# A hash-attention and gated feed-forward kernel: third pair's loads on the SP ring, a dummy matmul per step of the first block, one more PSUM copy on VectorE, the last output tile in two halves

## The chip, the cores and the metric

The kernel runs on one core of a Trainium2 chip. The metric is the device time of one execution in microseconds (us). A profiled span, which is what the trace covers, is about 2 us shorter than the time of the same execution. Each execution also reports the mean clock that the throttle granted to TensorE (1.0 is full speed).

Executions of one kernel do not agree here to a fraction of a per cent. In three sets of timed runs of the kernel before (157 executions) they lie between 359.7 and 368.2 us, and the mean clock goes with it: some 360.9 us where it is above 0.9925, 362.5 near 0.99, 364.3 near 0.98. Executions more than 1.5% above the fastest of the same kernel are labelled slow (48 of the 157); the ratios below use the fast ones only. The slow ones of the kernel before are, with few exceptions, those with the lowest clocks (0.959 to 0.984), so leaving them out also leaves out part of what a steadier clock is worth.

## The reference

```python
# q, k, v: (4, 8, 768, 64); proj: (64, 6)
q_bucket = sum over bits of ((q @ proj) > 0) * 2**bit        # the same for k
mask = q_bucket[..., :, None] == k_bucket[..., None, :]
attn = softmax(where(mask, q @ k.T / sqrt(64), -1e9))
x = (attn @ v), heads joined                                  # (3072, 512)
ffn = (gelu(x @ w_gate) * (x @ w_val)) @ w_out
out = x + sigmoid(x @ w_res) * ffn                            # (3072, 512), float32
```

## The kernel before

Attention works through 16 pairs of heads (4 batches by 4 pairs). For a pair, q and k are transposed on TensorE (tiles `tps`), hashed by small matmuls (`hps`), and the signs are written by VectorE (`bits`). Seven "hash rows" per operand are then moved by DMA under the scaled q and k in the tile `aug`, so that a score matmul over 64 + 7 = 71 rows gives a large negative number where the hashes differ. A step is two score matmuls (`sc`), one exp on ScalarE (`e`), and six matmuls with v (`av`, over 65 columns). 24 steps make a block; six steps belong to one pair. After each block comes the feed-forward of its tokens, whose matmuls fill TensorE during the next block. The first block has nothing to fill it with.

```python
    load_pair(1, nc.sync, "qk")          # SP ring
    load_pair(0, nc.sync, "v")
    load_pair(1, nc.sync, "v")
    ...
    def prep_pair(n):                    # pairs 1 to 3
        for g in range(3):
            ps = mm_psum.tile([P, 512], FP32, tag="mm", name="tps")
            for i in range(4):
                nc.tensor.transpose(ps[:, i * P:(i + 1) * P], tiles[4 * g + i], ident)
            if g == 1 and n > 1:
                nc.vector.tensor_copy(trT[:, g * 512:(g + 1) * 512], ps)
            else:
                nc.scalar.copy(trT[:, g * 512:(g + 1) * 512], ps)
            yield True
        ...                              # hash matmuls, bits on VectorE
        for i in range(4):               # the hash rows, by DMA
            eng = nc.sync
            eng.dma_start(a[D:KAUG, i // 2, (i % 2) * S:(i % 2 + 1) * S], bits[32 * i:32 * i + NR])
        ...
    prep_first()
    cast_v(0)                            # GpSimd: v of pair 0 to bf16
    load_pair(2, nc.gpsimd)              # the third pair
    prep = prep_pair(1)
    ...
    load_pair(3, nc.gpsimd)
    cast_v(1)
    for _ in range(KM):
        run(weights)                     # GpSimd issues weight loads; more at pairs 2 and 3
    for i in range(NS + LEAD):
        scores(i)                        # cut: conditions
        ...                              # attend(i - 2), prepare, feed-forward pieces
```

`mm_psum` has three buffers (in PSUM, where this kernel's matmuls write and ScalarE and VectorE read) for all transposes, hashes and feed-forward products; the last output tile is 12 matmuls of 512 columns, two VectorE operations and one DMA.

## Time and profile before

| | before |
|---|---|
| median time of three executions | 363.50 us (361.92 to 363.65) |
| profiled span, mean clock | 362.8 us, 0.971 |
| TensorE busy | 350.9 us, 97% |
| score step 6, step 12, step 18 start | 21.78, 29.35, 34.72 us |
| gate matmuls (`gps`) of the first block follow each other without a wait ("run free") from | 45.08 us |
| from there to the last matmul's start | 312.5 us |
| last matmul's end to the end of the span | 4.85 us |

The last four rows split the span into a head, a middle and a tail. In the middle TensorE is busy nearly throughout (312.78 of 312.91 us in this profile), and it is the same to 0.3 us in ten of the fourteen profiles of this study (312.5 to 312.8 us; the other four are those with weights held back); head and tail are where the time can move. The prediction below shows the lines that this rests on. In the chain of waits, a line is the start in us, the length in us, and what the chain went through: an instruction, a transfer (DMA), or "issue". In the tables of stretches the columns are the stretch, its length, the busy time of PE, PEld, DVE, ACT and POOL with instruction counts, the granted clock, and the DMA share and GB/s.

### The profile page before, as it was taken

How to read it: one execution, taken by the hardware profiler on the slowest of the kernel's cores; microseconds unless marked ns; L12 is line 12 of the kernel's file. 1: busy time of each engine (PE TensorE's matmuls, PEld its weight loads, DVE VectorE, ACT ScalarE, POOL GpSimd, SP SyncE). 2: the span in 40 equal slices, each digit the busy share in tenths (PEclk: the TensorE clock that was granted, in tenths of full speed). 3: DMA queues.
4: the chain of work that ended last, by engine and by line, in shares of the span. 5: the costliest groups of instructions: out<-in, count | busy, mean ns of one | idle time of the engine just before them, and what ended most of it. 6: DMA issues, size and time to landing. Idle time of an engine off the chain costs nothing.

```text
span 362.8 us, 7661 instructions
## 1 busy us (share of the span) xinstructions
PE 350.9 (97%) x3094; PEld 207.2 (57%) x3094; DVE 184.1 (51%) x321; ACT 244.6 (67%) x349; POOL 27.9 (8%) x41
## 2 busy tenths in 40 slices
PE   7798999999999999999999999999999999999994
PEld 3455656555655556655565556655566556655651
DVE  4654206877287652856266562856253323524343
ACT  6567787556865678675886678675887778776310
POOL 0963001000000000000000000000000000000000
PEclk9787599999999999999999999999999999999999
DMA  7699999798027678009820669000100010001001
GB/s 244 200 240 215 216 169 158 125 152 132 29 45 98 108 136 113 1 28 165 130 37 7 107 131 117 3 22 33 44 2 1 31 60 0 3 31 58 2 12 75
DMA packets 104330, 31.54 MB, mean 87 GB/s; under 512 B 95284, under 2 KB 99720, under 8 KB 104296
## 3 DMA queue, kind: packets, MB, share of 16 engines
q1 hardware_dynamic: 100040, 23.27, 36.9%
q0 software_dynamic: 3952, 7.60, 10.0%
q8 instruction: 24, 0.39, 0.5%
q10 hardware_dynamic: 304, 0.20, 0.2%
q14 instruction: 10, 0.08, 0.1%
HBM read 29.36 MB, written 6.29 MB: 98 GB/s over the span
## 4 chain that ended last, share of the span: by engine, by line
PE 92%; issue 3%; DMA 3%; ACT 1%; DVE 1%; POOL 1%; SPq 0%; POOLq 0%; DVEq 0%; ACTq 0%
PE sc L285 18%; PE vps L347 17%; PE gps L337 17%; PE ops L362 17%; PE av L305 10%; PE rps L355 6%; PE hps L223 4%; PE xps L327 2%; DMA aug<-bits 1%; DMA ks<-in_k_dram 1%; PE tps L192 1%; ACT e L288 0%; PE hps L242 0%; POOL qs L82 0%; ACT xT L330 0%
## 5 line engine op out<-in xcount | busy, mean ns | idle before, releaser
L288 ACT ACTIVATE e<-sc 128x768 bf16<-128x768 f32 x192 | 152.5, 810 | 63.6 <-PE sc L285 63.1
L285 PE MATMUL sc<-aug 71*128 71x384 bf16 x384 | 97.6, 340 | 1.5 <-DMA aug<-bits 1.1
L350 DVE TENSOR_TENSOR gh<-vps,gh 128x384 bf16<-128x384 f32 x96 | 52.8, 551 | 81.0 <-PE vps L347 62.9
L347 PE MATMUL vps<-xT,wv 128*128 128x384 bf16 x384 | 75.3, 326 | 0.0
L305 PEld LDWEIGHTS <-e 128*128 128x128 bf16 x1152 | 59.6, 101 | 25.2 <-issue 4.4
L362 PE MATMUL ops<-wo,gh 128*128 128x512 bf16 x288 | 71.9, 379 | 0.0
L305 PE MATMUL av<-vaug,e 128*128 128x65 bf16 x1152 | 64.6, 198 | 0.8 <-DVE xtok L315 0.8
L337 PE MATMUL gps<-xT,wg 128*128 128x384 bf16 x384 | 64.6, 327 | 0.1
L285 PEld LDWEIGHTS <-aug 71*128 71x128 bf16 x384 | 36.7, 101 | 33.5 <-issue 5.7
L339 ACT ACTIVATE gh<-gps 128x384 bf16<-128x384 f32 x96 | 45.3, 490 | 11.4 <-PE gps L337 10.2
L337 PEld LDWEIGHTS <-wg 128*128 128x128 bf16 x384 | 37.6, 98 | 26.6 <-DMA wo<-in_moe_w_out_dram 0.7
L347 PEld LDWEIGHTS <-wv 128*128 128x128 bf16 x384 | 33.1, 98 | 20.6 <-issue 3.7
L367 DVE SCALAR_TENSOR_TENSOR y<-th,ops 128x512 f32<-128x512 bf16 x24 | 16.5, 686 | 45.6 <-PE ops L362 36.7
L362 PEld LDWEIGHTS <-gh 128*128 128x128 bf16 x288 | 25.0, 98 | 23.0 <-issue 1.2
L180 POOL CAST vaug<-vs 128x768 bf16<-128x768 f32 x16 | 13.3, 830 | 192.1 <-DMA vs<-in_v_dram 98.9
L358 ACT ACTIVATE th<-rps 128x512 bf16<-128x512 f32 x24 | 14.3, 597 | 17.3 <-PE rps L355 17.3
L355 PE MATMUL rps<-wr,xT 128*128 128x512 bf16 x96 | 24.7, 380 | 0.0
L235 DVE TENSOR_SCALAR aug<-trT 64x1536 bf16<-64x1536 f32 x24 | 23.4, 976 | 0.3
L228 DVE TENSOR_SCALAR bits<-hps,shift 128x384 bf16<-128x384 f32 x24 | 13.7, 613 | 13.6 <-PE hps L223 13.6
L315 DVE TENSOR_TENSOR xtok<-av,rec 128x384 bf16<-128x384 f32 x32 | 17.8, 558 | 1.1
L369 DVE SCALAR_TENSOR_TENSOR o<-y,xtok 128x512 f32<-128x512 f32 x24 | 16.6, 692 | 0.8
L330 ACT COPY xT<-xps 128x768 bf16<-128x768 bf16 x8 | 6.4, 798 | 12.5 <-PE xps L327 12.5
(54 smaller groups left out, 160.6 us busy)
## 6 DMA issues: line engine op xcount, KB each, us to landing
out_dram<-o SPq DMA_DIRECT2D x24, 256.0 KB
vs<-in_v_dram SPq DMA_DIRECT2D x14, 384.0 KB
qs<-in_q_dram SPq DMA_DIRECT2D x48, 96.0 KB
ks<-in_k_dram SPq DMA_DIRECT2D x48, 96.0 KB
wg<-in_moe_w_gate_dram POOLq DMA_DIRECT2D x4, 384.0 KB, 9.4
wv<-in_moe_w_val_dram POOLq DMA_DIRECT2D x4, 384.0 KB, 13.9
wo<-in_moe_w_out_dram POOLq DMA_DIRECT2D x4, 384.0 KB, 16.4
aug<-bits SPq DMA_DIRECT2D x60, 10.5 KB
```

Of the source, the lines that this page charges most:

```text
L235: nc.vector.tensor_scalar_mul(a[0:D, hh, :], trT[hh * D:(hh + 1) * D].rearrange("d s n -> d (s n)"), QKS)
L285: nc.tensor.matmul(sp[:, x, 0:CH], a[:, S + jt * P:S + (jt + 1) * P], a[:, c * CH:(c + 1) * CH], start=True, stop=True)
L288: nc.scalar.activation(e, sp[:, :, 0:CH], AF.Exp, scale=EXPS)
L305: nc.tensor.matmul(av[:, o:o + D + 1], e[:, x, t * P:(t + 1) * P], va[:, 2 * j + hh, TS[b][jt], :], start=(first and x == 0 and t == 0), s ...
L315: nc.vector.tensor_mul(x_tok[u][:, :, j * P:(j + 1) * P].rearrange("p t (h d) -> p h t d", h=2), o[:, :, :, 0:D], rec.to_broadcast([P, 2, ...
L337: nc.tensor.matmul(ps[:, 0:CH], wg[:, kk, m * P:(m + 1) * P], xT[u][:, kk, :], start=(kk == 0), stop=(kk == KM - 1))
L339: nc.scalar.activation(gh[u][:, m, :], ps[:, 0:CH], AF.Gelu)
L347: nc.tensor.matmul(ps[:, 0:CH], wv[:, kk, m * P:(m + 1) * P], xT[u][:, kk, :], start=(kk == 0), stop=(kk == KM - 1))
L350: nc.vector.tensor_mul(sl, ps[:, 0:CH], sl)
L355: nc.tensor.matmul(rps, xT[u][:, kk, t * P:(t + 1) * P], wr[:, kk, :], start=(kk == 0), stop=(kk == KM - 1))
L362: nc.tensor.matmul(ops, gh[u][:, kk, t * P:(t + 1) * P], wo[:, kk, :], start=(kk == 0), stop=(kk == KF - 1))
L369: nc.vector.scalar_tensor_tensor(o, y, 0.5, x_tok[u][:, t, :], op0=ALU.mult, op1=ALU.add)
```

## The change

The intent: pair 2 arrives without waiting for GpSimd; a dummy matmul in each step is meant to keep the clock of TensorE up; one more PSUM copy per pair leaves ScalarE for VectorE; and the work after the last matmul is halved.

```diff
     load_pair(0, nc.sync, "v")
+    load_pair(2, nc.sync, "qk")
     load_pair(1, nc.sync, "v")
+    load_pair(2, nc.sync, "v")
...
-            if g == 1 and n > 1:
+            if g > 0 and n > 1:
                 nc.vector.tensor_copy(trT[:, g * 512:(g + 1) * 512], ps)
...
+            parts = 2 if u == 2 * B - 1 and t == TC - 1 else 1
+            W = DMODEL // parts
+            for h in range(parts):
+                cols = slice(h * W, (h + 1) * W)
...              (matmuls, the two VectorE operations and the DMA on these columns only)
     cast_v(0)
-    load_pair(2, nc.gpsimd)
     prep = prep_pair(1)
...
+        if i < LB and i >= LEAD:
+            busy = mm_psum.tile([P, 512], FP32, tag="mm", name="busy")
+            nc.tensor.matmul(busy, warm[:, 0:P], warm, start=True, stop=True)
```

More of the change, by code (lines that the diff above doesn't have):

```diff
@@ L359, in feed_forward @@
             yield 0.87
-            ops = mm_psum.tile([P, 512], FP32, tag="mm", name="ops")
-            for kk in range(KF):
-                nc.tensor.matmul(ops, gh[u][:, kk, t * P:(t + 1) * P], wo[:, kk, :],
-                                 start=(kk == 0), stop=(kk == KF - 1))
-                if kk % 4 == 3 and kk < KF - 1:
-                    yield 0.87
-            y = o_pool.tile([P, DMODEL], FP32, tag="y", name="y")
-            nc.vector.scalar_tensor_tensor(y, th, 1.0, ops, op0=ALU.add, op1=ALU.mult)
-            o = o_pool.tile([P, DMODEL], FP32, tag="o", name="o")
-            nc.vector.scalar_tensor_tensor(o, y, 0.5, x_tok[u][:, t, :], op0=ALU.mult, op1=ALU.add)
-            lay = "(p t) d -> p t d" if b == 0 else "(t p) d -> p t d"
-            nc.sync.dma_start(
-                out[b * S:(b + 1) * S, :].rearrange(lay, t=T)[:, TS[b][c * TC + t], :], o)
+            parts = 2 if u == 2 * B - 1 and t == TC - 1 else 1
+            W = DMODEL // parts
+            for h in range(parts):
+                cols = slice(h * W, (h + 1) * W)
+                ops = mm_psum.tile([P, 512], FP32, tag="mm", name="ops")
+                for kk in range(KF):
+                    nc.tensor.matmul(ops[:, 0:W], gh[u][:, kk, t * P:(t + 1) * P], wo[:, kk, cols],
+                                     start=(kk == 0), stop=(kk == KF - 1))
+                    if kk % 4 == 3 and kk < KF - 1:
+                        yield 0.87
+                y = o_pool.tile([P, DMODEL], FP32, tag="y", name="y")
+                nc.vector.scalar_tensor_tensor(y[:, 0:W], th[:, cols], 1.0, ops[:, 0:W],
+                                               op0=ALU.add, op1=ALU.mult)
+                o = o_pool.tile([P, DMODEL], FP32, tag="o", name="o")
+                nc.vector.scalar_tensor_tensor(o[:, 0:W], y[:, 0:W], 0.5, x_tok[u][:, t, cols],
+                                               op0=ALU.mult, op1=ALU.add)
+                lay = "(p t) d -> p t d" if b == 0 else "(t p) d -> p t d"
+                nc.sync.dma_start(
+                    out[b * S:(b + 1) * S, cols].rearrange(lay, t=T)[:, TS[b][c * TC + t], :], o[:, 0:W])
             yield 0.87
```

## The prediction

> **What bounds the kernel now.** I read the page first (engine shares, the 40 slices), then the chain of waits from 0 to 60 us, then a table of stretches cut where the granted clock changes, then the order of work between 10 and 45 us, then the DMA landings.
>
> ```profile
> PE 350.9 (97%) x3094; PEld 207.2 (57%) x3094; DVE 184.1 (51%) x321; ACT 244.6 (67%) x349; POOL 27.9 (8%) x41
> PE   7798999999999999999999999999999999999994
> PEclk9787599999999999999999999999999999999999
> ```
> TensorE is busy nearly everywhere, and from slice 6 on it is busy at full clock. In the first five slices (45 us, the first block, where no feed-forward work exists yet to fill TensorE) the granted clock is low. The changes touch only this head and the last tile; the 313 us between (45.08 us, where the first gate matmuls run freely, to 357.99 us, the last matmul) are TensorE-bound and stay.
>
> The chain of waits, first 60 us:
> ```profile
> 10.64 0.85 POOL qs L82
> 11.49 3.98 DMA ks<-in_k_dram
> 15.47 0.04 issue
> 15.52 0.47 PE tps L192
> ...
> 23.87 5.43 DMA aug<-bits
> 29.30 0.04 issue
> 29.35 0.51 PE sc L285 x2
> ...
> 42.81 1.40 PE xps L327 x12
> 44.21 0.02 issue
> 44.23 0.81 ACT xT L330
> 45.04 0.04 issue
> 45.08 1.79 PE gps L337 x10
> ```
> Pair 2 (the third) is loaded by GpSimd. GpSimd first casts pair 0's v, so it issues q only at 10.64 and k lands at 15.47: TensorE, ready at 12.43, waits. Later the hash rows of pair 2 take 5.43 us through the DMA queues before scores step 12 can start at 29.35.
>
> The stretches, cut at the clock's changes (columns: PE, PEld, DVE, ACT, POOL busy, then PEclk):
> ```profile
> 10.81:14.22 3.41, 1.62 (x19) 0.47 (x12) 3.32 (x5) 2.19 (x3) 3.41 (x5) 1.00 0.60 176
> 14.22:17.63 3.41, 3.02 (x21) 2.22 (x22) 0.63 (x1) 1.40 (x2) 3.41 (x6) 0.50 0.96 290
> 17.63:21.05 3.42, 3.42 (x31) 2.52 (x37) 0.69 (x1) 1.70 (x3) 2.86 (x5) 0.50 0.94 273
> ...
> 27.87:31.29 3.42, 2.09 (x26) 1.25 (x24) 3.02 (x5) 2.67 (x4) 2.24 (x2) 1.00 1.09 216
> 31.29:34.70 3.41, 3.19 (x30) 2.18 (x30) 0.08 (x1) 2.55 (x5) 0.77 (x1) 0.50 1.07 213
> ```
> Every change of clock lies on a grid of 3.41 us. The clock halves after a stretch with PE busy 1.62 of 3.41, and again after one with 2.09; it does not after 2.60 or 2.64. So there are two half-clock stages, 14.22 to 21.05 and 31.29 to 44.94. In the second, a score step takes 0.97 us (exps start at 34.67, 35.64, 36.61), though an exp needs only about 0.79 (three take 2.25 to 2.37): TensorE at half clock is the bound, ScalarE would be otherwise.
>
> [...] from 31.29 to 41.53 PE is shown busy 3.19, 3.41 and 3.41 of 3.41 and stays at 0.50. [...]
> [...] here the issuing engine decides when: the DMA rate is 154, 12, 0 and 101 GB/s in the four microseconds from 9 to 13, an empty queue that the SP ring can fill.
>
> **The change part by part.**
> *Loads of pair 2.* The landings of q1, k1, v0, v1 are 7.74, 8.80, 9.82 and 10.82 us, one per 1.03 us. With q2, k2 behind v0: q2 10.85, k2 11.9, v1 12.9, v2 14. All before use; TensorE goes on at 12.43 instead of 14.47 (2.04 saved) and the second wait (0.54 on k) goes. No stretch is then as empty as 10.81 to 14.22, so I expect no half clock from 14.22. GpSimd loses 2.3 us of issues, so pair 3 and the weights come that much earlier.
> *Copies of pairs 2 and 3, third group, from ScalarE to VectorE.* Two copies of 0.58 leave ScalarE, two of 0.69 go to VectorE, which has room except just behind its scaling ops (1.95 per pair).
> *Dummy matmul.* 22 of them, at full clock about 0.22 us each (a 512-column ops matmul repeats every 0.86/4 = 0.22), 4.8 us of TensorE. A warm step is 0.33 (sc) + 0.19 (av) = 0.52; with the dummy 0.74, still under the 0.79 of ScalarE. So it lies beside the exps. It also takes one of three PSUM buffers in each step; where the buffer held the tile of a DVE copy, the dummy waits for that copy.
> *Table of the block after the change,* step by step with these durations (transposes of a group 0.4, hash 0.9): sc3 at 13.2, sc4 14.6, sc5 15.85, hash of pair 2 16.4 to 17.3 (before: 20.97 to 21.85 at the end of the half clock). Then sc6 needs the hash rows of pair 1, issued from 12.9: before, the second of these DMAs landed at 20.21, behind the loads that were queued then. Afterwards the queue holds pairs 2 and 3 to about 17.1, so 17.3 to 19.5; I take sc6 at 18.4 (before 21.78). The bits of pair 2 at 18.5, second DMA issued 19.25, plus 5.43 as before gives 24.7; TensorE, held at one point by the DVE evacuation of av and once by the copy, reaches sc12 at 25.75 (before 29.35). From there ScalarE paces: 14 exps of 0.79 give the last at 37.3, with one hold of 0.6 for the hash rows of pair 3 (25.85 + 4.94 = 30.8 against sc18 at 30.2) 37.9; the transposes of x are warm, the ScalarE copy (0.81) follows at once: gates run from 38.85 instead of 45.08. **Gain 6.2 us**, of which 3.6 come before sc12 and 2.6 after.
> *Last tile in halves.* Twelve matmuls of 512 become 24 of 256: about +0.1 on TensorE. The two vector ops after the last matmul, 0.69 each, become some 0.42 each (an estimate: 128x384 takes 0.55, 128x512 0.69, so a column costs about 1.1 ns and the rest is fixed): 1.41 to 0.87, saved 0.54. The last output DMA (issued 359.54, landed 361.56) has half the bytes; [...] **Gain 0.8.**
> Sum: 7.0 us. 363.5 - 7.0 = 356.5.
>
> **The rivals.**
> 1. *The clock stays low or falls again.* If the wait at sc6 or sc12 empties a 3.41 us window, the clock halves, and each step then costs 0.97 + 0.43 (a dummy at half clock, the opening ones repeat every 0.43) = 1.4 instead of 0.97. For: the same kind of DMA wait preceded both drops. Against: the dummies raise the share, and TensorE is blocked under 1 us at a time in my table. One such window costs about 1.5 us, a whole block would eat all: 362 to 365.
> 2. *Hash rows take the place of the load wait.* The DMA queue is full from 12 to 48 us; if pair 1's rows land at 21.5 again (the fourth did before), sc6 does not move, and only the gain after sc12 and the tail stay: 2.6 + 0.8, so 360.
> 3. *It is hidden or better.* If the early DMA wait is shorter because pair 2 is already through, sc6 comes at 17.6 and the block follows by 1 us; and if the evacuations hold TensorE less than I put down, another 0.5: 355.
> 4. *The feed-forward of the first block is short of weights.* The last gate chunk landed at 29.62, last value chunk at 37.45 (used at 53), the last output weights at 48.51 (used at 72). Starting 6 us earlier is still later than each. Pair 4's k landed at 51.80, needed on VectorE at 62.09: 10 us of room. I give this little.
>
> **Range and chances.** Centre 356.4 (the table's 356.5, rivals 1 and 3 roughly even). The runs before spread over 1.7 us[...], so a range of 353.5 to 360.0. Two per cent is 7.3 us, just above my 7.0: faster by over 2% 0.43, within 2% 0.55, slower by over 2% 0.02.
>
> **What would show it.** Right: PEclk at 1.00 from 4 us on; no DMA wait of TensorE on q or k of pair 2; TensorE's first gate matmuls free-running near 38.9 us; exps from step 12 on at 0.79 to 0.84 each; the same 313 us from there to the last matmul; the time from last matmul to end 4.1 rather than 4.85. Wrong: half-clock stretches inside 12 to 38 us, a wait on the hash-row DMAs over 2 us at sc6 or sc12, steps longer than 0.9 with ScalarE idle (then the dummy or its buffer costs), or a new wait after 40 us.

## The result, and the profile after

The kernel after took 359.07 us (median of four, 358.23 to 360.29) against 363.57 for the kernel before: ratio 0.9882, 95% interval 0.9833 to 0.9931. A ratio is the mean time of one kernel's fast runs over that of the other's of the same rounds, so it is not quite the ratio of the medians. The control run later in the study gave 0.9923 (0.9893 to 0.9953). By the 2% measure that is "same", some 4 us faster, where 7 were forecast.

The page of the kernel after (busy shares; the busy tenths of TensorE and the granted clock in 40 slices):

```profile
PE 348.4 (97%) x3128; PEld 206.3 (58%) x3128; DVE 185.7 (52%) x325; ACT 242.9 (68%) x347; POOL 25.4 (7%) x38
PE   7889999999999999999999999999999999999995
PEclk9989999999999999999999999999999999999999
```

The clock is nearly full from the start; in this execution one dip is left, in the third slice. The chain of waits of the kernel after, first 60 us:

```profile
13.61 0.91 SPq L209
14.53 0.05 issue
14.57 5.43 DMA aug<-bits
20.00 0.05 issue
20.05 0.50 PE sc L287 x2
...
28.75 4.92 DMA aug<-bits
33.67 0.05 issue
33.72 0.50 PE sc L287 x2
...
40.91 0.81 ACT xT L332
41.72 0.04 issue
41.77 1.78 PE gps L339 x10
```

The wait for pair 2's k is gone. In its place stand the hash rows: those of pair 1, sent at 14.57, land 5.43 us later and hold step 6 until 20.05, and those of pair 3 hold step 18 until 33.72. The gate matmuls run free from 41.77 instead of 45.08. The stretch with the first of these waits, and the one after it:

```profile
18.24:21.65 3.41, 1.80 (x19) 1.21 (x19) 2.89 (x4) 1.00 (x2) 1.46 (x3) 1.00 1.09 215
21.65:25.06 3.41, 3.41 (x19) 2.51 (x18) 1.59 (x4) 1.81 (x3) 2.07 (x4) 0.50 1.09 216
```

TensorE was busy 1.80 of 3.41 us, and the clock was halved for the next 3.41 us. The long second fall of the kernel before, four windows from 31.29 us, is gone: the stretch with the hold at step 18 has 2.75 us of work, and the clock stays full.

```profile
31.89:35.30 3.41, 2.75 (x36) 1.68 (x34) 0.13 (x1) 2.57 (x5) 0.00 (x0) 1.00 1.26 208
```

Last, the tail, in order of time:

```profile
354.67 0.42 DVE L373 SCALAR_TENSOR_TENSOR y<-th,ops 128x256 f32<-128x256 bf16 x1 [0.36 <-PE ops L368]
355.12 0.43 DVE L376 SCALAR_TENSOR_TENSOR o<-y,xtok 128x256 f32<-128x256 f32 x1
```

The operations of the half tile take 0.42 and 0.43 us instead of 0.69 each; the last DMA, issued at 355.58, landed at 357.28 (1.70 us; the whole tile's took 2.02), and the span ends 3.68 us after the last matmul instead of 4.85.

### The profile page after: what moved, and what is told of

It reads as the page before. It is cut to its first block, busy times and chain, and to the rows that moved or that the text cites. A ratio compares the mean times of both kernels' runs of the same rounds, so it can differ in the third digit from the quotient of the medians.

```text
span 358.3 us, 7733 instructions
## 1 busy us (share of the span) xinstructions
PE 348.4 (97%) x3128; PEld 206.3 (58%) x3128; DVE 185.7 (52%) x325; ACT 242.9 (68%) x347; POOL 25.4 (7%) x38
## 4 chain that ended last, share of the span: by engine, by line
PE 91%; DMA 4%; DVE 2%; SPq 1%; ACT 1%; issue 0%; ACTq 0%
PE vps L349 18%; PE gps L339 18%; PE ops L368 17%; PE sc L287 16%; PE av L307 9%; PE rps L357 6%; PE hps L225 4%; DMA aug<-bits 3%; PE xps L329 1%; DMA ks<-in_k_dram 1%; DVE aug L268 1%; PE tps L194 1%; PE busy L460 1%; DVE bits L204 1%; SPq L209 0%
## 5 line engine op out<-in xcount | busy, mean ns | idle before, releaser
L287 PE MATMUL sc<-aug 71*128 71x384 bf16 x384 | 93.3, 326 | 3.3 <-DMA aug<-bits 2.3
L368 PE MATMUL ops<-wo,gh 128*128 128x512 bf16 (+1 forms) x300 | 71.9, 371 | 0.0
L307 PEld LDWEIGHTS <-e 128*128 128x128 bf16 x1152 | 56.7, 97 | 21.5
L307 PE MATMUL av<-vaug,e 128*128 128x65 bf16 x1152 | 61.7, 194 | 0.0
L373 DVE SCALAR_TENSOR_TENSOR y<-th,ops 128x512 f32<-128x512 bf16 (+1 forms) x25 | 16.6, 665 | 46.1 <-PE ops L368 37.2
L368 PEld LDWEIGHTS <-gh 128*128 128x128 bf16 x300 | 26.1, 98 | 22.1 <-issue 1.2
L376 DVE SCALAR_TENSOR_TENSOR o<-y,xtok 128x512 f32<-128x512 f32 (+1 forms) x25 | 16.9, 674 | 0.9
```

Source lines behind the costliest of these rows:

```text
L287: nc.tensor.matmul(sp[:, x, 0:CH], a[:, S + jt * P:S + (jt + 1) * P], a[:, c * CH:(c + 1) * CH], start=True, stop=True)
L307: nc.tensor.matmul(av[:, o:o + D + 1], e[:, x, t * P:(t + 1) * P], va[:, 2 * j + hh, TS[b][jt], :], start=(first and x == 0 and t == 0), s ...
L368: nc.tensor.matmul(ops[:, 0:W], gh[u][:, kk, t * P:(t + 1) * P], wo[:, kk, cols], start=(kk == 0), stop=(kk == KF - 1))
L376: nc.vector.scalar_tensor_tensor(o[:, 0:W], y[:, 0:W], 0.5, x_tok[u][:, t, cols], op0=ALU.mult, op1=ALU.add)
```

## The experiments

All runs below gave correct results. "Full clock" counts executions with a mean clock of 0.998 or more. One window of 3.41 us at half clock takes 3.41 x 0.5 / 357 = 0.0048 off the mean, so 0.995 is one such window, 0.990 two, 0.981 four. Medians are of all executions; ratios are of fast ones. The three groups are three sets of runs, each with its own runs of the kernel before (medians 363.97, 364.11 and 363.37 us).

| run | what | median (range), us | ratio, 95% interval | full clock |
|---|---|---|---|---|
| e1_no_dummy | after, no dummies | 360.28 (358.85 to 363.79) | 0.9946, 0.9916 to 0.9976 | 0 of 22 |
| e2_loads_pool | after, pair 2 from GpSimd | 361.89 (359.43 to 364.57) | 0.9972, 0.9941 to 1.0004 | 7 of 22 |
| e4_rows_dve | after, hash rows copied by VectorE | 364.33 (363.06 to 365.13) | 1.0046, 1.0019 to 1.0072 | 3 of 11 |
| e9_weights_late | after, weights held to 28 us | 364.39 (363.47 to 365.96) | 1.0060, 1.0024 to 1.0096 | 0 of 8 |
| after_again | after | 359.85 (357.77 to 363.34) | 0.9923, 0.9893 to 0.9953 | 11 of 19 |
| e3_halves_alone | before + halves | 361.49 (358.17 to 367.26) | 0.9934, 0.9905 to 0.9962 | 1 of 22 |
| e6_loads_alone | before + SP loads | 363.35 (359.13 to 365.83) | 0.9980, 0.9950 to 1.0010 | 0 of 22 |
| e12_weights_after_rows | after, weights held for the rows of pair 2 | 358.57 (357.64 to 359.03) | 0.9890, 0.9856 to 0.9924 | 6 of 6 |
| e5_dummy_alone | before + dummies | 362.55 (359.91 to 365.44) | 0.9998, 0.9974 to 1.0023 | 6 of 22 |
| e7_copy_back | after, third copy on ScalarE | 359.53 (357.27 to 363.92) | 0.9917, 0.9881 to 0.9952 | 9 of 14 |
| e12_again | as e12 | 358.63 (358.00 to 359.36) | 0.9909, 0.9878 to 0.9939 | 6 of 6 |
| e13_gated_no_dummy | e12 without dummies | 360.28 (359.01 to 362.30) | 0.9952, 0.9934 to 0.9970 | 0 of 22 |

The theory: the missing part of the gain is the wait for hash rows, which stand behind weight data on the DMA engines. Rivals: the missing part is the clock; or the dummies take as much as they give; or a 5 us landing is simply what such a DMA takes.

### Without the dummies (e1_no_dummy)

```diff
-        if i < LB and i >= LEAD:
-            busy = mm_psum.tile([P, 512], FP32, tag="mm", name="busy")
-            nc.tensor.matmul(busy, warm[:, 0:P], warm, start=True, stop=True)
```


> The kernel after, without the 22 dummy matmuls; loads, copies and tail halves stay. Theory (the dummies hold the granted clock at full rate in the first block, and their own time lies beside the exps): the clock falls to half in the stretch where score steps wait for the exps or for hash rows, steps there take 0.97 us instead of 0.73, the first gate matmuls run free 2 to 3 us later than with dummies (41.8 in the profiled run), mean clock 0.96 to 0.98, time 361 to 362 us. Rival (the dummies cost what they give, because they take PSUM buffers and TensorE time): 358 us or less, and the clock full.

No execution of 22 kept the full clock (0.981 to 0.990, two to four windows), where 11 of 19 of the kernel after did. The profiled one lost one window from 21.61 us, after a wait of 3.62 us for hash rows at step 6, and three from 35.26 us, after the wait at step 18; its gates ran free from 44.74 us. The median of 360.28 is better than the 361 to 362 expected. The rival, which had the clock staying full, is out; how much time the dummies are worth is measured better by e13 below, since here the two intervals overlap.

### Pair 2 from GpSimd again (e2_loads_pool)

```diff
-    load_pair(2, nc.sync, "qk")
-    load_pair(2, nc.sync, "v")
     cast_v(0)
+    load_pair(2, nc.gpsimd)
```


> The kernel after, but pair 2 is loaded by GpSimd as before; dummies, copies and tail halves stay. Theory (the early loads take away 2 us of waiting for pair 2, but half of it comes back as the wait for hash rows at score step 6): pair 2's q lands at 14.4 again, step 6 starts near 20.5 to 22 instead of 20.05, so the loss is only 0.5 to 1.5 us: 359.5 to 360.5. Rival (the early loads are worth their full 3.6 us of landing): 362 or more.

The time rises to 361.89, more than the expected 359.5 to 360.5 and near the rival's 362. Two profiled executions that both had the full clock show what the early loads do step by step: the hash of pair 2 starts at 19.09 with GpSimd loads and at 16.87 in the control of the kernel after, 2.2 us earlier. Step 6 starts at 20.23 and 20.11: nearly all of the 2.2 us has gone into the wait for pair 1's hash rows. What is left shows later. VectorE has scaled pair 2 by 23.1 and 21.4 us, so it copies pair 3's transposes earlier, and pair 3's hash, which needs these copies, is over 0.7 us earlier: step 12 at 27.50 and 26.78, gates free from 41.38 and 40.44, 0.9 us. The times agree: the executions at full clock average 359.99 us here (7) and 358.97 in the control (11), 1.0 apart. The medians of the two differ by 2.0; the clock, full in 7 of 22 here and in 11 of 19 there, goes with the rest. The two come from two sets, run on two chips, so the split is an estimate.

### Hash rows copied by VectorE (e4_rows_dve)

```diff
-            eng = nc.sync
-            eng.dma_start(a[D:KAUG, i // 2, (i % 2) * S:(i % 2 + 1) * S], bits[32 * i:32 * i + NR])
+            nc.vector.tensor_copy(a[D:KAUG, i // 2, (i % 2) * S:(i % 2 + 1) * S],
+                                  bits[32 * i:32 * i + NR].rearrange("r p n -> r (p n)"))
```


> The kernel after, with the hash rows of pairs 1 to 3 copied into place by VectorE (four copies of 7 partitions by 768 columns per pair) instead of by DMA. Theory (the wait for the hash-row DMAs, 1.6 us at step 6 and 0.7 at step 18, is where the missing part of the gain went): both waits vanish from TensorE's list, and if a copy takes 0.3 us the time falls to 356.0 to 357.5. If a copy takes 0.8 us, VectorE is filled by 3.3 us more per pair and the gain is lost in waits for VectorE. Rival (the rest is the clock, not the rows): no change from 358.8.

The DMA waits vanish, and the time is worse than before the change: the 356.0 to 357.5 expected for a copy of 0.3 us was a miss. A copy took 0.35 us, so four add 1.4 us per pair; but they stand ahead of the scaling of q and k and of the PSUM copies on VectorE, and the scaling ran slower (1.24 us median instead of 0.96). Waits from 10 to 40 us (total, times, longest):

```profile
PE av L307 <- DVE xtok L317: 3.5, 2, 2.3
PEld hps L244 <- DVE trT L196: 3.2, 3, 2.3
```

TensorE now waits for VectorE; step 12 starts at 30.82 instead of 26.78 in the full-clock profile of the kernel after. This does not test the rival, because a new bound took the place of the wait; it shows that VectorE has no room there.

### Weights held back (e9_weights_late)

```diff
+        if i == 14:
+            late = s_pool.tile([P, 1], BF16, tag="late", name="late")
+            nc.gpsimd.tensor_copy(late, x_tok[0][:, 0, P:P + 1])   # waits for pair 1's x
+            drain(weights)                                         # all weight loads; the earlier calls are taken out
```


> The kernel after, but GpSimd issues all weight loads only after the second pair's rows of x are written (about 27 us instead of 13), so that the queues are empty when the hash rows of pairs 1 and 2 are sent. Theory (hash rows take 5.4 us because they stand behind weight data on the same DMA engines): issue to landing falls to 2 to 3 us for pairs 1 and 2, step 6 starts at 18.5 without a wait, the first gate matmuls 1.5 to 2.5 us earlier if the gate weights arrive in time (issued 27 + 8 to 10 us = 37), time 356.5 to 358. Rival (5 us is what such a small DMA takes in any case): landing unchanged, time as after or, with the gate waiting for weights, worse.

The chain of waits:

```profile
18.41 0.49 PE sc L287 x2
...
29.71 9.68 DMA wg<-in_moe_w_gate_dram
39.39 0.05 issue
39.44 6.58 PE gps L339 x29
```

Step 6 starts at 18.41 without a wait. The second row DMA of pair 2, issued at 20.21, landed at 22.11, and that of pair 3, issued at 26.02, at 27.93: 1.9 us each, where the kernels before and after show 4.9 to 5.4 for the same transfers. So 5 us is not what such a DMA takes; it takes that behind weight data. The attention part of the block ended 2.2 us earlier than in the full-clock profile of the kernel after (x is transposed from 35.98 instead of 38.16). The kernel as a whole is slower, and its trace shows the weights now late: the last gate weights landed at 39.39, and pair 4's loads, behind the rest of the weights, kept a VectorE transpose waiting 3.4 us later on. The middle grew from 312.6 to 320.2 us. The expected 356.5 to 358 was a miss for that reason, which the expectation itself had named.

### The kernel after once more, and two parts alone (after_again, e3_halves_alone, e6_loads_alone)

> The kernel after once more, unchanged, as the control for the other runs of this call and because it had only four executions. Theory (its clock seldom falls, so it scatters less than the kernel before, whose executions lie between 359.7 and 368.2 us with the mean clock): median 358.5 to 359.5, mean clock 0.995 or more in most executions, ratio 0.984 to 0.989. Rival (the four executions were lucky): median 360 or more.

The median is 359.85 and the ratio 0.9923, the clock full in 11 of 19. The expected 358.5 to 359.5 (ratio 0.984 to 0.989) was a miss; the result lies beside the rival's 360, so the four first executions were somewhat lucky. With the four first executions that makes 14 of 23; these average 358.93 us, the other eight fast ones 361.5. In the profiled one, at full clock, step 6 still starts at 20.11, after TensorE stood still for 1.91 us, and the gates run free from 40.44.

> The kernel before, with only the last output tile in two halves. From the traces: last matmul to the end of the span 4.85 us before and 3.7 us in the kernel after, so 0.9 to 1.2 us less, in every clock state: 362.7 to 363.2 beside 363.9 of the kernel before. Rival (the extra weight loads take it back): under 0.3 us.

Its edit is the halving part of the change alone. The span ended 3.84 us after the last matmul, 1.0 less than before. The time fell by more, 2.4 us by the ratio, where about 1 was expected. The clock can account for the surplus: seven of the 22 count as slow and are left out, and the fast ones that remain have a mean clock of 0.989, where those of the kernel before have 0.983. At 1.9 us for 0.01 (the slope over all 157 executions of the kernel before) that is 1.1 us, an estimate. Nothing in the edit touches the first block, so this looks like luck. In all eleven profiles with the halves the last matmul is followed by 3.65 to 3.90 us, in the three without by 4.64 to 4.85.

> The kernel before, with only pair 2's loads moved to the SP ring (no dummies, copies as before, last tile whole). Theory (the early loads move the work before step 6 forward by some 2 us, as the run with GpSimd loads and all else changed lost 2 to 3 us): 361.5 to 362.5, mean clock 0.97 to 0.99[...]. Rival (all of the early landing is taken back by the wait for hash rows): 363.5 or more.

Its edit is the SP loads alone. The ratio of 0.9980 does not tell it from the kernel before; the medians are 363.35 and 364.11. In its profile pair 2's hash starts at 16.41 (before: 20.97), yet step 6 at 20.29 after waiting for rows, and two falls of the clock follow. The expected 361.5 to 362.5 was a miss, and the result lies beside the rival's 363.5: of the 4.6 us by which the hash came earlier, 1.5 are left at step 6 (before: 21.78) and 0.8 at the gates (44.27).

### Weights held only until pair 2's rows have landed (e12_weights_after_rows, e12_again)

```diff
+        if i == 8:
+            late = s_pool.tile([P, 1], BF16, tag="late", name="late")
+            nc.gpsimd.tensor_copy(late[D:D + 1], aug_of(0, 2)[D:D + 1, 0, S:S + 1])   # waits for the rows
+            drain(weights)                       # all weight loads; the earlier calls are taken out
```


> The kernel after, with the weight loads held until the hash rows of pair 2 have landed (about 21 us; the run with the loads held to 28 us landed the rows in 1.9 us instead of 5.4, but then waited 1.7 us and more for gate weights and 3.4 us for pair 4). Theory (the rows' wait behind weight data is the missing part of the gain): no wait at steps 6 and 12, pair 3's rows still 4 to 5 us, first gate matmuls 1.5 to 2.5 us earlier than in the kernel after, no wait for gate weights (the last lands near 34 us), pair 4 in time: 356.5 to 357.8. Rival (the weights or pair 4 come too late again): 359 or more, with a wait on those DMAs after 38 us.

> The kernel after with the weight loads held until pair 2's hash rows have landed, once more: it had six executions. Theory: 358.0 to 359.0, clock 0.998 to 1.0 in nearly all executions, so it scatters less than the kernel after (357.8 to 363.3). Rival (six lucky executions): 360 and a clock of 0.995 in half of them.

The chain of waits of the first run:

```profile
18.00 0.49 PE sc L287 x2
...
25.62 5.32 DMA aug<-bits
30.98 0.50 PE sc L287 x2
...
51.81 4.65 DMA ks<-in_k_dram
56.49 0.99 DVE trT L220
```

Steps 6 and 12 start at 18.00 and 25.27 without waiting (20.11 and 26.78 in the full-clock profile of the kernel after). Pair 3's rows, again behind weights, take 5.32 us and hold step 18 to 30.98, as the theory says. The gates run free from 39.03 (second run: 39.05) instead of 40.44. The middle is 0.6 to 1.1 us longer, because pair 4's k now lands at 56.5, just too late. In the same set the fast runs average 358.49 us against 360.01 of the kernel after, and all 12 executions of the two runs had a clock of 0.998 or more and lie within 1.7 us. The gates came 1.4 us earlier where 1.5 to 2.5 were expected, and with the longer middle the median missed the expected range by 0.8 us; the repeat, at 358.63, lies in its own expected range.

What the held weights buy is mainly a steady clock. Where the clock is full in both, little is left: 358.49 against 358.97 us (11 executions) of the kernel after in the first set, and in the second 358.60 for both this version and the full-clock executions (9) of the copies back on ScalarE, which is the kernel after but for one copy. So of the 1.4 us at the gates, at most 0.5 shows in the time at full clock. With the steadiest clock and the lowest mean of all executions, this version is the best of the study.

### Dummies alone, and held weights without dummies (e5_dummy_alone, e13_gated_no_dummy)

> The kernel before, with only the 22 dummy matmuls. Theory (the dummies keep the clock at full rate wherever TensorE is not simply stopped by a DMA): mean clock 0.99 to 1.0 where the kernel before has 0.978, so by the slope of the kernel before (1.9 us for 0.01) 2 to 3 us less: 361 to 362.5. Rival (dummies matter only after the early loads have removed the stop at pair 2): clock as before, 363.5 or more.

The edit is the `busy` matmul alone. The mean clock rises as expected (median 0.995, kernel before 0.984), but the ratio of fast runs is 0.9998: no gain, and the expected 361 to 362.5 was just missed. Those fast runs of the kernel before leave out 15 of 51, nearly all its executions with the lowest clock; the means of all executions differ by 1.0 us. At like clocks the dummies look costly here: eight executions at 0.994 to 0.995 average 362.80 us, eight of the kernel before at 0.993 and above 361.10. So the rival that the dummies take as much as they give is not out for this kernel, and no run tells where they would cost. Its profile shows what they do not prevent (stretches):

```profile
12.30:15.72 3.42, 1.77 (x15) 0.69 (x7) 3.38 (x5) 1.80 (x3) 3.42 (x5) 1.00 0.91 297
15.72:19.13 3.41, 3.10 (x21) 2.31 (x22) 0.48 (x1) 1.40 (x2) 3.41 (x6) 0.50 0.99 357
19.13:22.54 3.41, 3.25 (x44) 1.96 (x43) 1.21 (x2) 2.01 (x3) 2.23 (x4) 1.00 1.06 217
```

The wait for pair 2 leaves 1.77 us of work in a window and the clock falls, dummies or not. It is back after one window; that happens without dummies too (in the profiles of the halves alone and the SP loads alone), and no run tells why it is quick here. What is missing is the second fall: after 19.13 the clock of this profile stays full to the end of the work.

> The kernel with held weight loads, without dummies. Theory ([...] with only the wait at step 18 left, half-clock windows become rarer but a step without a dummy fills only 0.52 of 0.76 us, so the clock still falls in many executions, 0.985 to 0.995): 359.5 to 361. Rival A (without waits the dummies are not needed): equal to the held weights with dummies, 358.5. Rival B (light steps alone lower the clock every time): 0.98 and 361.5 or more.

```profile
29.68:33.09 3.41, 1.28 (x20) 0.90 (x19) 0.00 (x0) 1.44 (x3) 1.21 (x2) 1.00 1.09 209
33.09:36.50 3.41, 3.25 (x31) 2.00 (x30) 0.75 (x2) 2.68 (x4) 1.33 (x2) 0.50 1.14 211
36.50:39.92 3.42, 3.42 (x34) 2.40 (x32) 0.20 (x2) 2.93 (x4) 0.22 (x1) 0.50 1.15 212
39.92:43.33 3.41, 3.28 (x17) 1.73 (x15) 1.02 (x2) 2.54 (x4) 0.00 (x0) 0.50 1.34 198
```

The same stretch with dummies (e12_again), where the wait at step 18 is 0.80 us:

```profile
30.28:33.69 3.41, 2.68 (x29) 1.64 (x30) 0.75 (x2) 2.52 (x4) 0.83 (x2) 1.00 1.09 205
33.69:37.10 3.41, 3.31 (x52) 2.38 (x50) 0.12 (x1) 3.31 (x6) 1.49 (x2) 1.00 1.14 213
```

This is the clean test of the dummies: the same set, all executions fast, only the dummies differ. Without them the clock is halved after the wait at step 18 (2.12 us here), and it stays halved for three windows although TensorE is shown busy throughout. 22 of 22 executions lost two to four windows, and their mean is 360.34 us against 358.60 with dummies: 1.7 us. Rival A is out. Of rival B, the fall in every execution came true and the time of 361.5 did not; time and clock are where the theory had them.

Over all profiles of the study, the five kernels without dummies (before, e1, e3, e6, e13) each show a fall between 31.3 and 36.1 us that lasts two to four windows; of the nine profiles with dummies none does, and only the one whose gates waited for weights falls after 26 us at all while it has work.

### The copies back on ScalarE (e7_copy_back)

```diff
-            if g > 0 and n > 1:
+            if g == 1 and n > 1:
```


> The kernel after, with the third transpose group of pairs 2 and 3 copied by ScalarE again. Theory (in the stretch with transposes the exps are not the pace; the hash rows are, and ScalarE takes the copy before VectorE would, since VectorE is still scaling pair 1): hash of pair 2 not later than in the kernel after, 0.3 us to either side: 359.5 to 360.5, within the noise. Rival (ScalarE's 1.2 us come back in full): 361 or more.

The ratio is 0.9917, that of the kernel after in the set before 0.9923. The moved copies are worth nothing that these runs can show. The profile shows something else:

```profile
18.84 0.50 PE L287 MATMUL sc<-aug 71*128 71x384 bf16 x2 [1.30 <-DMA aug<-bits]
```

Step 6 starts 1.3 us earlier than in the control of the kernel after, and the gates run free from 39.49 instead of 40.44. The copies of pairs 2 and 3 come too late to matter for pair 1's rows; but GpSimd, later with its casts of v, issued its first weight load at 14.97, after the second row DMA (14.47) and not before it, and that DMA took 4.3 us. In the run without dummies, with weights issued from 13.49, it took 7.1 us. So the wait at step 6 differs by over 2 us between single profiles of nearly the same kernel, and small differences of it prove nothing; the big one, between weights before and after the rows, points the same way as the held weights.

## Why the prediction was right or wrong

Right in direction and in most parts, and its likeliest outcome, a change within 2%, came true; its size, 7.0 us, was too large by about 2.5 to 3. By its steps:

- **Loads of pair 2: right.** q, k and v landed at 10.16, 11.21 and 13.27 (forecast 10.85, 11.9, 14), before use, and the hash of pair 2 started at 16.68 and 16.87 (forecast 16.4, before 20.97).
- **Step 6: the term that failed.** "The queue holds pairs 2 and 3 to about 17.1, so 17.3 to 19.5; I take sc6 at 18.4." Measured 20.05 and 20.11, behind rows that landed at 20.00 and 20.06. The forecast had itself written that the weights come 2.3 us earlier, and did not carry that to the rows: weight loads were issued from 13.09 on, before the second row DMA at 14.57. With those weights held, step 6 started at 18.00 to 18.41, which is what the forecast had without them. This is the forecast's second rival in part: 1.7 us of it came true. TensorE stood still for 1.60 and 1.91 us there, where the table had it blocked for under 1 us at a time.
- **Step 12:** forecast 25.75, measured 28.36 with a half-clock window on the way and 26.78 without; held weights gave 25.27.
- **Step 12 to the gates: nearly right.** Forecast 13.1 us, measured 13.41 and 13.66; before it was 15.73. The hold at step 18 was put at 0.6; at full clock the three steps before it took 3.43 us instead of the 2.2 of unheld ones, so 1.2. The steps took less than forecast in return, 0.73 us instead of 0.79. So the dummies lay beside the exps as worked out.
- **The clock: half right.** "I expect no half clock" held in 14 of 23 executions. That dummies would hold the clock was the author's supposition; with the weights held, it was full in 6 of 6 executions with them (e12_again) and in 0 of 22 without (e13). The first rival holds for the rest, and its estimate of 1.5 us for a window is below the 2.5 us by which those executions differ; part of that difference may be the DMA landings that brought the fall about. The forecast's own sign of being wrong, a half-clock stretch inside 12 to 38 us, is in the first profile (21.65 to 25.06).
- **Copies: no effect measurable,** where the forecast had them relieve ScalarE. The expectation of that run argued that ScalarE is not the pace where they happen; no run shows it.
- **Last tile: too small.** 0.8 forecast, 1.2 measured (4.85 to 3.65 to 3.68). Of the 0.8, 0.54 was for VectorE; the rest, for a last DMA of half the bytes, was the author's estimate. The VectorE part was right, 0.42 and 0.43 us; TensorE's 24 half matmuls took 2.78 us where the 12 whole ones took 2.75, and the last DMA took 1.70 us instead of 2.02.
- **The weights being too late, the fourth rival: rightly discounted.** The middle stayed at 312.6 us.
- **DMA rate:** in the profile before, the loads issued by SP moved 395 GB/s from 8 to 9 us and those issued by GpSimd 412 from 13 to 14.
- **The sum: taken from the wrong start.** The gains were read from a profiled execution that took 364.91 us, and subtracted from the median of 363.5. From 364.91 they give 357.9.

From the profile of the kernel before to the full-clock one after: head 45.08 to 40.44, 4.6 us (forecast 6.2); tail 1.2 (0.8); together 5.87 us with the middle, as the spans 362.84 and 356.97 say. So of the 2.4 us between the forecast of 356.5 and this execution (358.93), 1.4 come from the start of the sum and 1.6 from the head, less 0.4 from the tail, to about 0.2. The executions without the full clock, eight fast ones of 23, raise the median further. That early loads and dummies need each other is suggested by the traces, but the ratios of the parts alone (0.9934, 0.9980, 0.9998, product 0.991) do not show it: their product is the whole within the noise.

## What to carry to other kernels

When a transfer is moved forward, follow everything that moves forward with it: here the weight loads came ahead of small, urgent row transfers, which took 5.43 us to land (1.9 with the weights held, for those of pairs 2 and 3), and took back nearly all of the 2.2 us that the early load had won, until the next hold-up. A large load that is needed late can be held by a one-element read of what has to come first; here that steadied the clock more than it shortened the full-clock time, because a later load then came just too late. Dummy matmuls beside the exps were worth 1.7 us once the early holds were gone, and nothing measurable alone. They are no guard against a stop: the clock fell after a stop of 1.60 us at step 6 in one profile of the kernel after, and stayed full through one of 1.91 us in the other. With the stop at steps 6 and 12 taken away, all 12 executions kept the clock. When gains are summed, subtract them from the execution that they were read from, not from a median.

## What the runs show of the clock and of the row transfers

- Without dummies the clock stayed at 0.50 for windows in which TensorE is shown busy 3.25 of 3.41 and 3.42 of 3.42 us (held weights, no dummies). Why it stayed there was not shown.
- The clock fell after windows with 1.28 (held weights, no dummies), 1.62 and 2.09 us of work (kernel before), and no threshold on busy time fits all: in the control run of the kernel after it stayed full after 1.51 of 3.42 us, as the next line shows.

```profile
16.69:20.11 3.42, 1.51 (x23) 0.54 (x23) 2.46 (x5) 0.81 (x1) 2.95 (x6) 1.00 1.02 190
```

- A row transfer of seven rows mostly took about 5 us (4.3 to 7.1 for the second one of a pair) from issue to landing behind weight data, and 1.9 us with the weight loads held back (e9_weights_late).
- The scatter of the kernel goes with its clock: in the kernel before, 157 executions spread over 8.5 us, 2.3%, and 0.01 of mean clock went with 1.9 us.
